# Order of work in a fused attention and expert kernel: gate weights, key and query steps, and the planning of slot 0

## The chip, the cores and the metric

One core of a Trainium2 chip runs the whole kernel. Five engines run their own queues in order: PE (TensorE, matrix products and transposes through the identity; PEld are its weight loads), ACT (ScalarE), DVE (VectorE), POOL (GpSimd) and SP (SyncE, which here only issues loads). The metric is the device time of one execution in microseconds; the time of a kernel is the median of several runs.

## The reference, cut to what matters

```
# attention: 4 batches x 8 heads, 768 tokens, 64 wide; 8 memory keys and values per head
for c in range(24):                              # chunks of 32 queries
    k_ctx = k[:, :, max(0, 32*c - 16):min(768, 32*c + 40)]
    scores = q_c @ concat(mem_k, k_ctx).T / 8
    a = softmax(scores)
    out[:, :, chunk] = a @ concat(mem_v, v_ctx)
# experts: the result as 3072 tokens x 512, 8 experts, one chosen per token
x = out.transpose(0, 2, 1, 3).reshape(3072, 512)
logits = x @ w_gate + modality_bias[modality_id]
e = argmax(logits); gate = softmax(logits)[e]
y[token] = gate * (relu(x[token] @ w1[e]) @ w2[e])    # 512 -> 1024 -> 512
```

Everything is float32. Expert products are made of a high and a low part of each operand (fp32r), three products for each full one.

## The kernel before, in words

**Attention.** The 32 heads are taken as 16 pairs u, each pair in two half steps, so 32 steps i = 2u + hf, in a loop that is pipelined by hand (`for i in range(n + 2)`). Step i issues the scores of its own unit (L328), transposes, attends (L345, L357) and normalizes (L365 to L370) the unit before, and transposes the result of the unit before that into `xall` (L382, L385). In between stands the preparation of the next pair. In an even step: `trans_k` of both heads on PE (L310, L314), four key copies `store_k` on ACT (L320), the memory keys on POOL (L302), and `regroup_q`, a DVE copy of the next pair's queries (L277). In an odd step: `trans_q` of both halves on PE (L292) with two copies on ACT (L297), and `share_v`, which copies value rows that two chunks share, on POOL (L267). POOL also issues the stores of the attention's result (`store_x`, L375).

**Loads.** SP issues every load in program order: keys and queries of a pair (L93), values of a pair in three pieces per head (L254 to L256), memory rows (L263), and once four small loads with the gate weights (L170 to L173). `gate_weights` spreads the gate weights over a padded tile `wg` on POOL (L234, L235), `bias_rows` makes the bias rows (L238 to L242).

**Routing.** After each four pairs the batch is routed (`route`): gate logits on PE (L530), their transposition (L541, L542), ranks by matmuls (L572 to L577), then six pairs of one-hot tiles ("hot tiles", `l` L656 and `a` L659), of which the first two are made on POOL and the others on DVE, and six matmuls of them (L667) that give the table of places (L671). The gates `gt` (L615) go to a DRAM tensor `gd`: by POOL (L622) for most batches, by SP (L1098) for the third, amid slot 0's weight loads. The route is a generator: each `yield "v"` ends a step after one DVE instruction, and `pump` or `further` take so many steps at places of the program, so that its instructions are mixed into the engines' queues by where these calls stand. Of the last batch's route (`last`, taken on by `further`) four of six tiles are made on POOL, and the gates' store stands ahead of the third tile.

**Experts.** A slot is 256 tokens of one expert: tokens are fetched by indirect DMA (`gather`, L751), transposed (`trans`: PE L803, high part on ACT L805, low part on DVE L806), weights are split into high (ACT L741) and low (DVE L742) by `conv`, the first product is `mm1_first` (L830, L831, L832) and the second `mm2` (L842). Slot 0's result is scaled on ACT (L846) and scattered by two indirect DMAs on POOL (`store`, L847); `keep` (L745, L747) puts the places and gates of the next slot aside on POOL. During slot 0 the last batch's route runs with `plan_slots`, a chain of small DVE instructions (L445 to L470, with `plan_row` L422 to L442 in it) that distributes the tokens over the later slots. The transposes of slot 1 stand in the second product of slot 0, at f = 5 and 6.

```
    for f in range(8):              # second product of slot 0
        if f == 2: further(2, True)
        mm2("av", f)
        if f < 5: conv(11 + f)
        if f == 5: load_w(1, 1)
        if f in (5, 6): trans(f - 5)
        if f > 2:
            further(2)
            conv(f - 3)
    store(0)
```

Of the kernel before, what the change touches and what calls it, by code (L numbers as in the profile page):

```python
# [39 lines left out]
NVW = 3  # L40
ORDERED = {mybir.EngineType.PE, mybir.EngineType.SP, mybir.EngineType.Pool, mybir.EngineType.Activation, mybir.EngineType.DVE}
# [3 lines left out]
def tile_chunk_attention_top1_moe(  # L45
# [239 lines left out]
    def trans_q(u):  # L285
        qr = qrs.pop(u)
        for j in range(2):
            t = qts[u, j] = bank()
            if u == 1 and j == 0:
                warm(t, 5)  # L290
            for i in range(3):
                nc.tensor.transpose(t[:, i:3 * P:3], qr[:, 2 * i + j].rearrange("p h d -> p (h d)"), ident)  # L292
# [11 lines left out]
    def trans_k(u):  # L304
        k2 = k2s.pop(u)
        for h in (1, 0):
            hh = 2 * u + h
            t = kts[u, h] = bank()
            for i in range(3):
                nc.tensor.transpose(t[:, 9 + i:9 + i + 3 * P:3], k2[:, 3 * h + i, :], ident)  # L310

            pads = bass.AP(tensor=t.tensor, offset=t.offset + 1, ap=[list(t.ap[0]), [392, 2], [1, 8]])
            mem_sel = ident[:, 4 * hh:4 * hh + 4].unsqueeze(1).unsqueeze(1)
            nc.tensor.matmul(pads, mkp, mem_sel.to_broadcast([P, 2, 2, 4]), start=True, stop=True)  # L314
# [107 lines left out]
    def plan_row(pos, tail, pt):  # L422
# [8 lines left out]
        vec.tensor_mul(three[:, 1], three[:, 1], noth)  # L431
        vec.scalar_tensor_tensor(off, off, 2.0, col0u, op0=ALU.mult, op1=ALU.add)
# [12 lines left out]
    def plan_slots():  # L445
# [21 lines left out]
        vec.reduce_sum(row, plan_row(pcol[0:64], None, None), axis=AX.X)  # L467
# [4 lines left out]
    def plan_tails():  # L472
# [28 lines left out]
        vec.reduce_sum(row, plan_row(pos, tail, pt), axis=AX.X)  # L501
# [453 lines left out]
    for i in range(n + 2):  # L955
# [26 lines left out]
        if u + 1 < NU and hf == 0:  # L982
# [3 lines left out]
            if 0 < u < NU - 2:  # L986
                regroup_q(u + 1)
# [11 lines left out]
        elif u + 1 < NU:  # L999
# [6 lines left out]
            trans_q(u + 1)  # L1006
            store_q(u + 1, 0)
            store_q(u + 1, 1)
            pump(3)
# [47 lines left out]
        if i == 9:  # L1057
            gate_weights()
            bias_rows()
        if i == 5:  # L1060
            nc.scalar.copy(mvx[1][:, :, 0:D], mvn[:, 1:2].to_broadcast([P, NCH, D]))
        if i == n - 5:
            regroup_q(NU - 1)
# [12 lines left out]
        if (u, hf) == (NU - 2, 1):  # L1076
# [20 lines left out]
            with nc.allow_non_contiguous_dma(reason="one gate per token"):  # L1097
                nc.sync.dma_start(*chosen.pop())  # L1098
# [57 lines left out]
    for f in range(8):  # L1156
# [9 lines left out]
        if f > 2:  # L1166
            further(2)
            conv(f - 3)
# [158 lines left out]
```

## Time and profile before

| what | value |
|---|---|
| runs, us | 427.58, 426.6, 427.71; median 427.58 |
| profiled execution, us | 428.59, of which its span is 426.8 |
| busy, us and share | PE 407.6 (95%), PEld 342.6 (80%), DVE 334.1 (78%), ACT 298.6 (70%), POOL 238.6 (56%) |
| granted clock, mean | 0.992 |
| attention | 9 to 131 us; from there on the expert slots |
| slot 0, slot 1 | first product of slot 1 from 163.8 us |

Times in the trace count from the span's start. A row of a timeline is a run of like instructions on one engine: its start, its length, the line, what it writes and reads, how many, and in brackets how long the engine stood idle ahead of it and what ended that. The granted clock (PEclk) is 1 at full speed, 2.4 GHz, and 0.5 at 1.2 GHz. A wait on one engine costs time only if the end of the program hangs on it, which must be followed from engine to engine.

### The profile page before, as it was taken

What the parts mean: (1) busy time and instruction counts of PE and PEld (TensorE: products, weight loads), DVE (VectorE), ACT (ScalarE), POOL (GpSimd) and SP (SyncE); (2) the same over time, 40 slices, a digit from 0 to 9 for tenths busy, and PEclk for the clock granted to TensorE, in tenths of its full rate; (3) what the DMA queues carried; (4) which work ended last, traced back from release to release, by engine and by line L of the source; (5) the groups of instructions that cost most, each with busy time, mean ns of one, the idle gap of its engine ahead of it and who ended that gap; (6) DMA issues with size and microseconds to landing.
All of it is one profiled execution on the core that took longest, in us unless ns stands there. A gap on an engine that the chain in (4) does not pass through costs nothing.

```text
span 426.8 us, 11396 instructions
## 1 busy us (share of the span) xinstructions
PE 407.6 (95%) x3872; PEld 342.6 (80%) x3875; DVE 334.1 (78%) x788; ACT 298.6 (70%) x594; POOL 238.6 (56%) x320
## 2 busy tenths in 40 slices
PE   8899699999899999999999999999999999999993
PEld 5678478888776888989898887888888788888882
DVE  6989468879687878958979889768789787988750
ACT  7677667868685556746657677868878676888750
POOL 8886567668583445767754574354666266520101
PEclk9999999999999999999999999999999999999998
DMA  9899899999957920125423729979776514320101
GB/s 221 146 261 228 193 235 210 223 239 192 232 156 201 271 52 1 55 77 121 99 78 72 272 64 266 290 231 297 231 282 196 157 54 102 73 77 2 50 3 55
DMA packets 82543, 66.81 MB, mean 157 GB/s; under 512 B 50659, under 2 KB 71339, under 8 KB 82476
## 3 DMA queue, kind: packets, MB, share of 16 engines
q1 hardware_dynamic: 75276, 46.36, 45.0%
q0 software_dynamic: 6784, 19.50, 15.0%
q8 instruction: 33, 0.54, 0.5%
q14 instruction: 34, 0.28, 0.2%
q10 hardware_dynamic: 416, 0.13, 0.1%
HBM read 84.64 MB, written 12.76 MB: 228 GB/s over the span
## 4 chain that ended last, share of the span: by engine, by line
PE 71%; issue 12%; ACT 6%; POOL 4%; DVE 4%; DMA 2%; POOLq 0%; ACTq 0%
PE av L842 12%; PE tr L830 11%; PE sc L842 10%; PE tr L811 9%; PE av L357 5%; PE tr L814 5%; ACT kbd L320 4%; PE sc L328 4%; PE tr L382 3%; PE tr L345 2%; PE tr L292 2%; PE tr L310 2%; PE tr L530 2%; DMA out_dram<-o,ix_now 1%; POOL xg L751 1%
## 5 line engine op out<-in xcount | busy, mean ns | idle before, releaser
L811 PE MATMUL tr<-xt,w 128*128 128x512 f32 x256 | 70.1, 395 | 0.0
L742 DVE TENSOR_TENSOR w<-raw,w 128x512 fp32r<-128x512 f32 x96 | 64.7, 719 | 4.0 <-ACT w L741 3.2
L842 PE MATMUL av<-wh,h 128*128 128x512 f32 x192 | 61.5, 393 | 0.0
L267 POOL COPY vw<-vw 24x1472 f32<-24x1472 f32 x31 | 44.2, 1425 | 21.8 <-DMA vw<-in_v_dram 20.6
L741 ACT CAST w<-raw 128x512 fp32r<-128x512 f32 x96 | 53.9, 623 | 1.5 <-DMA raw<-in_moe_w_dram 1.5
L842 PE MATMUL sc<-wh,h 128*128 128x512 f32 x160 | 50.8, 392 | 0.0
L811 PEld LDWEIGHTS tr<-xt,w 128*128 128x128 f32 x256 | 44.3, 189 | 7.2 <-issue 0.8
L830 PE MATMUL tr<-xt,w 128*128 128x256 f32 x384 | 48.1, 284 | 0.7 <-DVE xt L806 0.7
L830 PEld LDWEIGHTS tr<-xt,w 128*128 128x128 f32 x384 | 46.8, 191 | 2.0 <-DVE xt L806 1.0
L320 ACT COPY kbd<-tr 64x672 f32<-64x672 f32 x57 | 44.5, 781 | 4.3 <-DVE kbd L320 2.3
L814 PEld LDWEIGHTS tr<-xt,w 128*128 128x128 f32 x256 | 39.2, 189 | 5.4
L847 POOL DMA_INDIRECT out_dram<-o,ix_now x22 | 26.1, 1184 | 29.6 <-ACT o L846 24.3
L842 PEld LDWEIGHTS av<-wh,h 128*128 128x128 f32 x192 | 36.0, 188 | 7.5 <-issue 0.2
L814 PE MATMUL tr<-xt,w 128*128 128x256 f32 x256 | 40.7, 281 | 0.0
L820 DVE TENSOR_TENSOR hs<-tr,hs 128x256 f32<-128x256 f32 x64 | 26.8, 419 | 17.6 <-ACT hs L817 17.6
L842 PE MATMUL av<-wl,h 128*128 128x512 f32 x96 | 37.5, 390 | 0.0
L821 ACT ACTIVATE h<-hs 128x256 fp32r<-128x256 f32 x64 | 26.8, 419 | 14.8 <-DVE hs L820 13.7
L751 POOL DMA_INDIRECT xg<-gd,gx x24 | 27.1, 1128 | 14.7 <-DMA gd<-gt 9.0
L842 PEld LDWEIGHTS sc<-wh,h 128*128 128x128 f32 x160 | 30.0, 188 | 6.3 <-issue 0.2
L823 DVE TENSOR_TENSOR wl<-vw,wh 128x512 fp32r<-128x512 f32 x48 | 33.2, 691 | 2.2
L824 DVE SCALAR_TENSOR_TENSOR h<-hs,h 128x256 fp32r<-128x256 f32 x64 | 27.7, 433 | 7.7 <-ACT h L821 7.3
L776 POOL COPY planes<-xg 128x1024 uint16<-128x1024 uint16 x18 | 24.0, 1339 | 17.0 <-DMA xg<-xd,gx 16.9
(266 smaller groups left out, 910.4 us busy)
## 6 DMA issues: line engine op xcount, KB each, us to landing
raw<-in_moe_w_dram SPq DMA_DIRECT2D x96, 256.0 KB
vw<-in_moe_w_dram SPq DMA_DIRECT2D x72, 256.0 KB
k<-in_k_dram SPq DMA_DIRECT2D x16, 384.0 KB
q<-in_q_dram SPq DMA_DIRECT2D x16, 384.0 KB
xd<-xb POOLq DMA_DIRECT2D x16, 384.0 KB
kbd<-in_moe_w_dram SPq DMA_DIRECT2D x24, 256.0 KB
vw<-in_v_dram SPq DMA_DIRECT2D x32, 184.0 KB
xall<-in_moe_w_dram SPq DMA_DIRECT2D x4, 1024.0 KB
```

Of the source, the lines that this page charges most:

```text
L267: copy(vw[r0:r0 + 24, h, 1:NCH, 0:D], vw[r0 + 32:r0 + 56, h, 0:NCH - 1, 0:D])
L320: copy(dst.rearrange("p c (i j) -> p c i j", j=2)[:, :, :, j], win)
L741: nc.scalar.copy(wh[i], raw[i])
L742: (eng or nc.vector).tensor_sub(wl[i], raw[i], wh[i].bitcast(F32))
L751: nc.gpsimd.indirect_dma_start(out=xg[t][:, part], out_offset=None, in_=rows, in_offset=bass.IndirectOffsetOnAxis(ap=gx[:, t:t + 1], axis=0))
L811: nc.tensor.matmul(ph, wh[f][:, c * P:(c + 1) * P], xt[:, c].rearrange("p a n -> p (a n)"), start=(c == 0), stop=False, skip_group_check=True)
L814: nc.tensor.matmul(ph[:, 0:256], wl[f][:, c * P:(c + 1) * P], xth[:, c], start=False, stop=(c == 3), skip_group_check=True)
L820: nc.vector.tensor_add(hs, ph[:, 0:256], hs)
L823: nc.vector.tensor_sub(wl[w], raw[w], wh[w].bitcast(F32))
L824: nc.vector.scalar_tensor_tensor(hl[:, f], hs, 0.0, hh[:, f].bitcast(F32), op0=ALU.max, op1=ALU.subtract)
L830: nc.tensor.matmul(ph, w[f][:, c * P:(c + 1) * P], x[:, c, :], start=(n == 0), stop=(n == 11))
L842: nc.tensor.matmul(pos[t], x, w[8 + f], start=(f == 0 and n == 0), stop=(f == 7 and n == 2))
```

## The change

It has four parts.

1. `gate_weights` and `bias_rows` are called at the end of step 8 instead of step 9.
2. From pair 6 on (`AHEAD = 5`), each step prepares one half of keys and one half of queries. The even step 2u makes the transposes and two copies of head 1's keys and of the queries' half 0, all of pair u + 1. The odd step 2u + 1 makes the queries' half 1 of pair u + 1, then the keys of head 0 of pair u + 2 with two copies, and `regroup_q` of pair u + 2. On PE an even step before had L310 and L314 twice and an odd one L292 for both halves; after, each step has L310 and L314 once and L292 for one half.
3. In slot 0's second product: `plan_row` ends a step in its middle (for `plan_slots` alone); at f = 5 one step of the route is taken instead of two; the subtraction of weight block 1 goes to POOL; blocks 2 and 3 are both converted at f = 6.
4. In slot 0's start the third batch's gates are stored by POOL instead of SP.

```diff
@@ -38,6 +38,7 @@
 NPOOL = 2
 NSPIN = 8
 NVW = 3
+AHEAD = 5
 ORDERED = {mybir.EngineType.PE, mybir.EngineType.SP, mybir.EngineType.Pool, mybir.EngineType.Activation, mybir.EngineType.DVE}
 
 
@@ -282,9 +283,9 @@
         for _ in range(k):
             nc.tensor.matmul(t, idle[:, 0:P], idle[:, P:640], start=True, stop=True)
 
-    def trans_q(u):
-        qr = qrs.pop(u)
-        for j in range(2):
+    def trans_q(u, js=(0, 1)):
+        qr = qrs[u]
+        for j in js:
             t = qts[u, j] = bank()
             if u == 1 and j == 0:
                 warm(t, 5)
@@ -301,9 +302,9 @@
             r = slice(64 * h, 64 * h + 64)
             eng.tensor_copy(kbds[u % 2][r, :, h, 56:64], memT[r, u:u + 1, :].to_broadcast([64, NCH, NMEM]))
 
-    def trans_k(u):
-        k2 = k2s.pop(u)
-        for h in (1, 0):
+    def trans_k(u, hs=(1, 0)):
+        k2 = k2s[u]
+        for h in hs:
             hh = 2 * u + h
             t = kts[u, h] = bank()
             for i in range(3):
@@ -419,7 +420,7 @@
         nc.vector.tensor_scalar(t, t, MAGIC, -MAGIC, op0=ALU.add, op1=ALU.add)
         return t
 
-    def plan_row(pos, tail, pt):
+    def plan_row(pos, tail, pt, step=None):
 
         vec = nc.vector
         full, sta, end = plan["full"], plan["sta"], plan["end"]
@@ -429,6 +430,8 @@
         vec.scalar_tensor_tensor(isf, end, pos, isf, op0=ALU.is_gt, op1=ALU.mult)
         vec.scalar_tensor_tensor(three[:, 1], off, 0.0, isf, op0=ALU.is_equal, op1=ALU.mult)
         vec.tensor_mul(three[:, 1], three[:, 1], noth)
+        if step:
+            yield step
         vec.scalar_tensor_tensor(off, off, 2.0, col0u, op0=ALU.mult, op1=ALU.add)
         vec.tensor_mul(three[:, 2], off, isf)
         if tail is not None:
@@ -464,7 +467,8 @@
         vec.scalar_tensor_tensor(sta, ohg[0:64], 2.0, sta, op0=ALU.mult, op1=ALU.add)
         vec.tensor_add(end, sta, left)
         row = plan_new("row", 3)
-        vec.reduce_sum(row, plan_row(pcol[0:64], None, None), axis=AX.X)
+        parts = yield from plan_row(pcol[0:64], None, None, "v")
+        vec.reduce_sum(row, parts, axis=AX.X)
         yield "v"
         vec.tensor_scalar(row[:, 2:3], row[:, 2:3], float(E * HI), None, op0=ALU.add)
         vec.tensor_copy(regs1, row)
@@ -498,7 +502,8 @@
         vec.tensor_scalar(pos, nfull, -32.0, tail_row, op0=ALU.add, op1=ALU.mult)
         vec.tensor_add(pos, pos, pcol[0:64])
         row = plan_new("row", 3)
-        vec.reduce_sum(row, plan_row(pos, tail, pt), axis=AX.X)
+        parts = yield from plan_row(pos, tail, pt)
+        vec.reduce_sum(row, parts, axis=AX.X)
         vec.tensor_scalar(row[:, 2:3], row[:, 2:3], float(E * HI), None, op0=ALU.add)
         vec.tensor_copy(regs, row)
 
@@ -979,11 +984,21 @@
                 nc.vector.tensor_copy(memT.rearrange("p u m -> p (u m)"), memp[:, 0:P])
                 load_mv(2)
             pump(1)
-        if u + 1 < NU and hf == 0:
+        if AHEAD <= u < NU - 1 and hf == 0:
+            if u < NU - 2:
+                mem_keys(u + 1, nc.gpsimd)
+            trans_k(u + 1, (1,))
+            pump(1)
+            store_k(u + 1, 1, 0, nc.scalar.copy)
+            store_k(u + 1, 1, 1, nc.scalar.copy)
+            trans_q(u + 1, (0,))
+            store_q(u + 1, 0)
+            pump(1)
+        elif u + 1 < NU and hf == 0:
             if 0 < u < NU - 2:
                 mem_keys(u + 1, nc.gpsimd)
             trans_k(u + 1)
-            if 0 < u < NU - 2:
+            if 0 < u < AHEAD:
                 regroup_q(u + 1)
             if u == 1:
                 blank_v(2)
@@ -1003,9 +1018,17 @@
                 share(u + 1, 0, nc.gpsimd.tensor_copy)
             else:
                 share_v(u + 1)
-            trans_q(u + 1)
-            store_q(u + 1, 0)
+            if u < AHEAD:
+                trans_q(u + 1)
+                store_q(u + 1, 0)
+            else:
+                trans_q(u + 1, (1,))
             store_q(u + 1, 1)
+            if AHEAD <= u + 1 < NU - 1:
+                trans_k(u + 2, (0,))
+                store_k(u + 2, 0, 0, nc.scalar.copy)
+                store_k(u + 2, 0, 1, nc.scalar.copy)
+                regroup_q(u + 2)
             pump(3)
         elif live:
             pump(3)
@@ -1054,13 +1077,11 @@
                 routing.append((route(u2 // 4), "tiled", u2 // 4, i))
         for _ in range(4 if i > 2 and hf == 1 else 0):
             next(constants, None)
-        if i == 9:
+        if i == 8:
             gate_weights()
             bias_rows()
         if i == 5:
             nc.scalar.copy(mvx[1][:, :, 0:D], mvn[:, 1:2].to_broadcast([P, NCH, D]))
-        if i == n - 5:
-            regroup_q(NU - 1)
         if i < n:
             pump(1, ("tiled",))
         if i < 2:
@@ -1095,7 +1116,7 @@
                 nc.gpsimd.memset(raw[f][0:1, 0:1], 0.0)
             load_w(0, 0, 1)
             with nc.allow_non_contiguous_dma(reason="one gate per token"):
-                nc.sync.dma_start(*chosen.pop())
+                nc.gpsimd.dma_start(*chosen.pop())
         elif (u, hf) == (NU - 1, 1):
             other = second()
             for f in range(8, 16):
@@ -1164,8 +1185,12 @@
         if f in (5, 6):
             trans(f - 5)
         if f > 2:
-            further(2)
-            conv(f - 3)
+            further(1 if f == 5 else 2)
+        if f in (3, 4, 7):
+            conv(f - 3, nc.gpsimd if f == 4 else None)
+        if f == 6:
+            conv(2)
+            conv(3)
     store(0)
 
     tails = plan_tails()
```

POOL around the gate weights; L267 are the copies of value rows, L375 the stores of the result, L302 the memory keys. Before:

```order
L302 COPY kbd_111<-memT 64x24x8 x2
L267 COPY vw_114<-vw_114 24x23x64 x2
L375 DMA xd<-xb 128x6x128
L234 MEMSET wg_135 128x480
L235 COPY wg_135<-wg 128x12x8
L238 MEMSET mods 25x128
L239 CAST mods<-mod_i 24x128
L240 TENSOR_TENSOR bias_b<-bias_b 24x8
L242 TENSOR_TENSOR rows_b<-bias_b,ident 24x192
L302 COPY kbd_110<-memT 64x24x8 x2
```

After, where line numbers are one higher in this part:

```order
L376 DMA xd<-xb 128x6x128
L303 COPY kbd_111<-memT 64x24x8 x2
L235 MEMSET wg_135 128x480
L236 COPY wg_135<-wg 128x12x8
L239 MEMSET mods 25x128
L240 CAST mods<-mod_i 24x128
L241 TENSOR_TENSOR bias_b<-bias_b 24x8
L243 TENSOR_TENSOR rows_b<-bias_b,ident 24x192
L268 COPY vw_114<-vw_114 24x23x64 x2
L376 DMA xd<-xb 128x6x128
```

The six instructions on gate weights and bias have moved ahead of one pair's value copies and result store.

POOL in slots 0 and 1, from the first hot tiles of the last batch on (L847 the scatters of slot 0's result, L622 the gates' store). Before:

```order
L656 TENSOR_SCALAR l_3162<-iota_147,lo 128x130
L659 TENSOR_SCALAR a_3163<-iota_148,ac,tokm 128x192
L656 TENSOR_SCALAR l_3166<-iota_147,lo 128x130
L659 TENSOR_SCALAR a_3167<-iota_148,ac,tokm 128x192
L622 DMA gd<-gt 128x6x4
L656 TENSOR_SCALAR l_3200<-iota_147,lo 128x130
L659 TENSOR_SCALAR a_3201<-iota_148,ac,tokm 128x192
L656 TENSOR_SCALAR l_3204<-iota_147,lo 128x130
L659 TENSOR_SCALAR a_3205<-iota_148,ac,tokm 128x192
L847 DMA out_dram<-o_3213,ix_now_171 3072x512
L847 DMA out_dram<-o_3218,ix_now_171 3072x512
L745 COPY ix_now_172<-ix 128x2
```

After; L661 and L664 are the hot tiles, L852 the scatters, L750 and L752 the copies of `keep`, L627 the gates' store:

```order
L747 TENSOR_TENSOR w_2583<-raw_2587,w_2582 128x512
L661 TENSOR_SCALAR l_3175<-iota_147,lo 128x130
L664 TENSOR_SCALAR a_3176<-iota_148,ac,tokm 128x192
L661 TENSOR_SCALAR l_3179<-iota_147,lo 128x130
L664 TENSOR_SCALAR a_3180<-iota_148,ac,tokm 128x192
L852 DMA out_dram<-o_3199,ix_now_171 3072x512
L852 DMA out_dram<-o_3204,ix_now_171 3072x512
L750 COPY ix_now_172<-ix 128x2
L752 COPY gate_now_174<-xg_2579 128x1
L752 COPY gate_now_174<-xg_2580 128x1
L627 DMA gd<-gt 128x6x4
L661 TENSOR_SCALAR l_3246<-iota_147,lo 128x130
```

A subtraction of weights stands ahead of the first two tiles, and the scatters, the copies and the gates' store ahead of the other two. The six matmuls on PE that take the tiles have kept their place, between the seventh and the eighth block of slot 1's first product.

DVE in the same stretch, from the first half's low part of slot 1's tokens on. Before, the second half's low part (the second L806) follows behind the plan, the third tile's inputs L629 to L640 and a subtraction L742, 19 rows further on; its last rows:

```order
L629 TENSOR_SCALAR h_3155<-rank 128x3x2
L632 TENSOR_SCALAR hi<-h_3155 128x6
L636 SCALAR_TENSOR_TENSOR lo<-hi,rank 128x6
L640 TENSOR_TENSOR ac<-c_3001,hi 128x6
L742 TENSOR_TENSOR w_2583<-raw_2588,w_2582 128x512
L806 TENSOR_TENSOR xt<-tr,xt 128x2x256
L610 TENSOR_REDUCE s_3186<-rex 128x3x2
```

After, from the first to the second half's low part (L811 for L806):

```order
L811 TENSOR_TENSOR xt<-tr,xt 128x2x256
L467 SCALAR_TENSOR_TENSOR sta<-ohg,sta 64x8
L468 TENSOR_TENSOR end<-sta,left 64x8
L428 TENSOR_SCALAR isf<-sta,pcol 64x8
L429 TENSOR_SCALAR off<-sta,pcol 64x8
L430 SCALAR_TENSOR_TENSOR isf<-end,pcol,isf 64x8
L431 SCALAR_TENSOR_TENSOR three<-off,isf 64x8
L432 TENSOR_TENSOR three<-three,noth 64x8
L811 TENSOR_TENSOR xt<-tr,xt 128x2x256
L435 SCALAR_TENSOR_TENSOR off<-off,col0u 64x8
```

The second half's low part stands in the middle of `plan_row`, ten rows earlier than the inputs of the hot tiles.

## Rows read from the trace of the kernel before

**Rows 1.** Timeline of PE: start us, us, what (out<-in, count), idle before and releaser.

```profile
51.44 2.78 PE L530 MATMUL tr<-xall,wg 128*32 128x256 f32 x24 [3.08 <-POOL wg L235]
53.98 1.30 PE L328 MATMUL sc<-kbd,qT 128*32 128x128 f32 x24
```

**Rows 2.** Timeline of PE in the second batch's step, same columns.

```profile
82.56 1.48 PE L530 MATMUL tr<-xall,wg 128*32 128x256 f32 x24
```

**Rows 3.** Windows: busy time per engine, then PEclk, DMA share, GB/s.

```profile
51.40:54.90 3.50, 3.46 (x44) 2.15 (x48) 0.00 (x0) 0.37 (x1) 2.53 (x7) 0.51 1.11 246
```

**Rows 4.** Timeline of GpSimd (POOL) around the gate weights.

```profile
46.64 3.10 POOL L267 COPY vw<-vw 24x1472 f32<-24x1472 f32 x2 [4.22 <-DMA vw<-in_v_dram]
...
51.12 0.27 POOL L235 COPY wg<-wg 128x96 f32<-128x96 f32 x1
```

**Rows 5.** Waits in 57 to 131 us: total, times, longest.

```profile
PEld tr L292 <- ACT kbd L320: 3.9, 8, 1.0
```

**Rows 6.** Timeline of SP's queue: small loads, queries, values, memory rows.

```profile
41.19 0.81 SPq L173 DMA_DIRECT2D rows_b<-n_moe_modality_bias_dram  x1
...
61.89 1.43 SPq L93 DMA_DIRECT2D q<-in_q_dram  x1
...
108.22 0.39 SPq L93 DMA_DIRECT2D q<-in_q_dram  x1
...
110.37 0.33 SPq L254 DMA_DIRECT2D vw<-in_v_dram  x1
...
112.05 2.89 SPq L263 DMA_DIRECT2D vw<-mvx  x2
```

**Rows 7.** Timeline of GpSimd at the attention's end.

```profile
116.57 2.88 POOL L267 COPY vw<-vw 24x1472 f32<-24x1472 f32 x2
...
124.45 1.00 POOL L659 TENSOR_SCALAR a<-iota,ac,tokm 128x192 fp32r<-128x192 f32 x1
```

**Rows 8.** Timeline of PE at the attention's end.

```profile
122.42 0.84 PE L328 MATMUL sc<-kbd,qT 128*32 128x128 f32 x24
...
126.10 0.91 PE L667 MATMUL tr<-a,l 128*128 128x192 f32 x6
```

**Rows 9.** Timeline of DVE at slot 1's start.

```profile
165.08 0.68 DVE L806 TENSOR_TENSOR xt<-tr,xt 128x512 fp32r<-128x512 f32 x1
```

**Rows 10.** Timeline of ACT at slot 1's start.

```profile
162.52 0.59 ACT L805 CAST xt<-tr 128x512 fp32r<-128x512 f32 x1 [0.67 <-PE tr L803]
```

**Rows 11.** Timeline of GpSimd in slot 1, whole up to the copies of keep.

```profile
164.59 1.06 POOL L656 TENSOR_SCALAR l<-iota,lo 128x130 fp32r<-128x130 f32 x1 [9.32 <-DVE ac L640]
...
167.25 1.30 POOL L659 TENSOR_SCALAR a<-iota,ac,tokm 128x192 fp32r<-128x192 f32 x1
168.50 0.93 POOL L622 DMA_DIRECT2D gd<-gt  x1
169.48 0.62 POOL L656 TENSOR_SCALAR l<-iota,lo 128x130 fp32r<-128x130 f32 x1
...
172.26 1.32 POOL L659 TENSOR_SCALAR a<-iota,ac,tokm 128x192 fp32r<-128x192 f32 x1
173.76 1.46 POOL L847 DMA_INDIRECT out_dram<-o,ix_now  x1 [0.18 <-ACT wh L741]
175.53 1.44 POOL L847 DMA_INDIRECT out_dram<-o,ix_now  x1 [0.30 <-ACT h L831]
...
177.09 0.31 POOL L747 COPY gate_now<-xg 128x1 f32<-128x1 f32 x2
```

**Rows 12.** Timeline of PE in slot 1, as far as the second expert product.

```profile
165.82 9.13 PE L830 MATMUL tr<-xt,w 128*128 128x256 f32 x74 [0.74 <-DVE xt L806]
174.79 0.82 PE L667 MATMUL tr<-a,l 128*128 128x192 f32 x6
175.56 1.70 PE L830 MATMUL tr<-xt,w 128*128 128x256 f32 x12
```

**Rows 13.** Line 847 (the scatters): duration ns, least, middle and longest.

```profile
L847 POOL DMA_INDIRECT out_dram<-o,ix_now x22: 982/1042/2695, 173.8 to 399.9; - x22
```

## The prediction

> **What bounds the kernel now.** I read the table of engines first, then PE's timeline, then what PE waits for. From 165 us to the end of the expert layers PE is never idle for as much as half a microsecond but once, so whatever PE loses or gains there goes into the end time one to one. In the attention part (9 to 131 us) there is one large hole: the gate logits of the first batch (L530) start after 3.08 us of idle, waiting for the gate weights that GpSimd spreads out at L235 [rows 1]. The hole has a second half. In the 3.5 us behind it the granted clock is 0.51, the lower of the two levels, 1.2 GHz [rows 3]; the same logits take 2.78 us there and 1.48 us in the second batch, the scores behind them 1.30 us and elsewhere 0.84 us [rows 1, 2, 8]. So the hole costs 3.08 + 1.30 + 0.46 = 4.8 us where it stands, with a few tenths more in the transposes between: 5.0 us.
>
> Two other things pace the attention, and they decide what becomes of these 5.0 us. First the loads: SP issues the queries of pair 9 at 61.89 and those of pair 15 at 108.22, 46.33 us for six pairs, 7.72 us a pair [rows 6]. SP does so when the loads before have landed, not when PE has used something, so a faster PE does not bring them forward. Second GpSimd's queue at the end: copy of pair 14's value rows, then the first two hot tiles of the third batch, which end at 125.45, and at 126.10 PE's table matmuls L667 take them [rows 7, 8].
>
> **Gate weights one step earlier.** In before, L234 to L242 stand on GpSimd behind the value copies of pair 5, which waited 4.22 us for their load and ran until 49.74 [rows 4]. After, they stand ahead of these copies. The last of the small loads was issued by SP at 41.19 [rows 6]. If it takes no longer than queries do (6.1 us, next part), the six instructions, 2.1 us in the trace (50.56 to 52.64), could end at 49.4 at the latest, and by the size of the load far sooner; PE is ready for L530 at 51.44 - 3.08 = 48.36. I take it that they are ready in time. The copies of pair 5 may come up to 2.1 us later, and a result store behind them; the step that attends with them comes two steps behind the hole, so nobody waits. Local gain at L530: 5.0 us, of which the slow case would leave 4.
>
> **Where the gain goes.** Queries of pair 15 bound how far PE can be ahead at step 29: SP's second load of the memory rows (two in the row that starts at 112.05 and ends at 114.94, 0.65 us each) starts when they are in, at 114.3, that is 6.1 us after their issue [rows 6]. Regrouping, transposes and copies take 2.7 us more, so the scores at 122.42 [rows 8] may come at 117.0: PE keeps 5.4 us at most there, the 5.0 and what the loads leave of the second part. But PE then meets L667 of the third batch, and that waits for GpSimd. Pair 14's second value load was issued at 110.37; at the 6.1 us that the queries took it is there at 116.5, its copy ends at 117.9 instead of 119.45, 1.5 us earlier, and everything behind it on GpSimd (a store, the expert choice that SP's weight loads wait for, the hot tiles) is 1.5 us earlier too: hot tiles done at 123.95, L667 at 124.05 instead of 126.10. That is **a gain of 2.0 us**. If the load is no earlier than the copy shows, PE still takes L667 right at 125.45: 0.65 us. If GpSimd's chain did not bind: 5.4 us. I take 2.0, by the load next to it in the queue.
>
> **Keys and queries spread evenly.** PE and ACT do the same work in other steps. What it can free is PE's wait for the key copies in odd steps, 3.9 us in 57 to 131 [rows 5]. The even spread needs each pair's queries one step (3.5 us) sooner. As the loads set the pace, I cost it at nothing by itself: its gain stands under the 5.4 us above and is cut by GpSimd in the same way. If the loads did not hide it, up to 3.9 us.
>
> **Second tile's split amid the planning.** PE waits 0.74 us at 165.82 for DVE's split of the second half (L806 at 165.08), which stands behind the whole of the planning [rows 9, 12]. ACT's part of the split ends at 163.11 [rows 10], so L806 can now run at 163.11 to 163.79. The wait and its 0.2 us of weight loading go: **0.95 us gained**. The price is what has been queued past it. On DVE, L640 has the 0.7 us of L806 ahead of it [rows 9], and so the first hot tile, which started at 164.59 when L640 was done [rows 11], starts at 165.3. On GpSimd two hot tiles come first as before, but then both scatters of slot 0's result (L847) and the two copies of keep, then the gates' store, and only then hot tiles 2 and 3, for which L667 on PE waits, with slot 1's whole remainder behind it. Step by step, on before's time axis:
> - hot tiles 0 and 1: 3.96 us [rows 11], 165.3 to 169.3;
> - two scatters: 1.46 and 1.44 us there, with 0.3 between [rows 11], but 1.04 in the middle of all 22 [rows 13]; 2.1 to 3.2, I take 2.5, to 171.8;
> - copies 0.45, gates' store 0.93 [rows 11], to 173.2;
> - hot tiles 2 and 3: 4.10 us as they stand [rows 11]; but PE has stopped by then and DVE with it, and the shorter L656 took 0.62 [rows 11] and the shorter L659 1.00 [rows 7], 3.24 us for two tiles. I take 3.3, to 176.5.
>
> PE comes to L667 at 174.79 - 0.95 = 173.84 [rows 12], does two of six, and waits. Four of six are left, 4/6 of the 0.82 us of that row, 0.55: PE is back at its experts at 177.05, and was at 175.56 [rows 12]: **1.5 us lost, net of the 0.95 gained**. With all instructions at their shorter values (3.96, 2.1, 1.4, 3.24) the tiles end at 175.3 to 176.0 and the loss is 0.25 us at the least; with all at the longer ones they end at 177.95, and it is 2.95. The subtraction that goes to GpSimd stands ahead of the hot tiles, in 9.32 us of idle [rows 11], and PE needs it only at 165; I cost it at nothing. Were it as long as 3 us it would still end before 165.3.
>
> On the length of the tiles the trace shows 1.00 us for L659 at 124.45, in the attention, and 1.30 and 1.32 us at 167.25 and 172.26, where DVE subtracts weights [rows 7, 11]. The Trainium skill, page "SBUF — State Buffer", section "Who interferes with whom", says that a VectorE instruction with two inputs in SBUF and a GpSimd one that reads SBUF exclude each other, the later waiting. By that rule the subtractions still queued at 173 us would keep the longer values for tile 2, and the loss would be some 0.4 us more.
>
> **Gates' store on GpSimd in slot 0.** It leaves SP's queue between the weight loads and takes 0.93 us on GpSimd, like the store of [rows 11], between short memsets that free SP's next loads. No instruction of PE waits for these within several microseconds. Cost and gain: nothing; with that cover gone it would be GpSimd's 0.93 us against, and as much for SP's earlier loads.
>
> **Sum.** -2.0 + 1.5 = -0.5 us. The profiled execution took 428.59 us, 1.0 above the median of the runs, and 1.8 above its own span; by the profiled one the forecast is 428.1, by the median 427.58 it is **427.1**, and that is the number I give.
>
> **Rivals.**
> (a) Slower: GpSimd's queue in slot 1 keeps the longer values, PE stands for some 3.9 us in two pieces, and the clock falls as it did after 3.08 us in one piece [rows 1, 3]. Price: 2.95, and 3.5 x 0.49 = 1.7 for the clock [rows 3], less 2.0: +2.65, 430.2. It decides where PE's idle before L667 passes about 3 us, hot tile 3 ending after 177.2. For it: every duration in rows 11 is one of this place. Against it: a short piece of matmul lies between the two waits, and DVE runs dry. The Trainium skill, "TensorE: Matmul & The Clock Gate", Part 1, says that the array's clock is halved when PE has been little busy and comes back when it is busy again; by that rule the clock's loss is real only in a long wait, which is why this case carries it and the forecast does not. Chance 0.22.
> (b) Faster: GpSimd does not bind at 124 us because pair 14's values are there earlier than any row says, and the whole of PE's 5.4 us arrives. -5.4 + 1.5 = -3.9, 423.7. For it: the copies of pair 14 ran without a pause, so their load may have been there long before. Against it: the loads' pace of 7.72 us a pair. Chance 0.15.
> (c) The attention gives only 0.65 us: pair 14's load is as late as the copies allow. +0.85, 428.4. Chance 0.12.
> (d) The third part does what it says and no more, no new wait at L667: the scatters need GpSimd only for a fraction of the time their rows show. -2.0 - 0.95 = -2.95, 424.6. Against it: the rows' sums. Chance 0.10.
>
> **How the numbers follow.** The forecast, 427.1, has 0.41, with own ends of 1.25 below and 1.45 above by the bounds of scatters and tiles. About 0.3% (1.3 us) is what a measurement of this kernel can tell from no change. Of the forecast's 0.41, 0.11 fall under 426.3, 0.27 within, 0.03 above; (a) is slower but for 0.03; (b) faster; (c) within but for 0.03; (d) faster but for 0.01. Faster 0.11 + 0.15 + 0.09 = 0.35, slower 0.03 + 0.19 + 0.03 = 0.25, the same 0.40. The range reaches down to (b) and up to (a), 423.8 to 430.2, which leaves out about half of each of the two.
>
> **What the changed profile would show.** Right: L530 of the first batch without a wait and no low clock at 51 us; PE waits for GpSimd's L659, 2 to 3 us in all, at the third batch's L667 near 122 us; no wait for L806 at slot 1's start, and 2 to 3 us at the last L667, with L847 ahead of L656 on GpSimd. Wrong: no wait at either L667 (then b or d), a low granted clock at 175 us (a), or SP's cadence of pairs under 7.3 us, which would mean that PE and not the loads set it.

## The result, and the profile after

The changed kernel takes 428.12 us (median of 18 runs) where the kernel before takes 426.37 us in the same comparison (18 runs); the ratio is 1.0051, with a 95% interval of 1.0026 to 1.0076. It is **slower by about 2 us**: 2.2 by the ratio, 1.75 by the medians; the ratio is taken over the fast runs alone (it leaves out two of the changed kernel's 18), and is not the quotient of the medians. The forecast was 0.5 us faster. The profiled execution took 427.23 us, 1.4 us less than the profiled one of before, so the two profiles show the opposite of the medians. Single executions of one kernel differ by 3 us and more, and a stage has to be compared over several of them.

The page of the changed kernel; PEclk is the granted clock in 40 slices, tenths of full speed:

```profile
span 425.4 us, 11403 instructions
...
PE 407.5 (96%) x3875; PEld 345.6 (81%) x3875; DVE 340.6 (80%) x787; ACT 301.3 (71%) x594; POOL 239.4 (56%) x322
...
PEclk9899999999999999699999999999999999999999
```

The 6 in the middle is the slice around 175 us. The low clock at 51 us of [rows 3] is gone, and a longer one has come at slot 1.

First the hole that the first part was to close. PE's timeline at the gate logits (start us, us, what; no bracket: no wait), which answers to [rows 1, 2]:

```profile
48.46 1.48 PE L535 MATMUL tr<-xall,wg 128*32 128x256 f32 x24
```

GpSimd's timeline at the gate weights, which answers to [rows 4]:

```profile
42.67 0.26 POOL L236 COPY wg<-wg 128x96 f32<-128x96 f32 x1 [0.67 <-DMA wg<-in_moe_w_gate_dram]
```

The gate weights are spread 5.5 us before PE asks for them, and the logits run at full speed.

PE's timeline in slot 1, which answers to [rows 12], with the first product, the six table matmuls L672 (L667 before) and the start of the second product:

```profile
156.24 8.80 PE L835 MATMUL tr<-xt,w 128*128 128x256 f32 x72
165.40 1.68 PE L835 MATMUL tr<-xt,w 128*128 128x256 f32 x12 [0.36 <-DVE h L837]
167.41 0.44 PE L672 MATMUL tr<-a,l 128*128 128x192 f32 x2 [0.33 <-DVE h L837]
169.73 0.35 PE L672 MATMUL tr<-a,l 128*128 128x192 f32 x1 [1.88 <-POOL a L664]
171.31 0.95 PE L672 MATMUL tr<-a,l 128*128 128x192 f32 x3 [1.22 <-POOL a L664]
172.06 2.81 PE L835 MATMUL tr<-xt,w 128*128 128x256 f32 x12
174.67 0.63 PE L847 MATMUL sc<-wh,h 128*128 128x512 f32 x1
```

Before, slot 1's first product and its second product started here:

```profile
163.72 1.36 PE L830 MATMUL tr<-xt,w 128*128 128x256 f32 x10
...
177.09 0.40 PE L842 MATMUL sc<-wh,h 128*128 128x512 f32 x1
```

The wait of 0.74 us for L806 is gone, but PE waits 0.36 and 0.33 us for DVE's low parts of h (L837) instead, and comes to the table matmuls no earlier: 11.17 us after the slot's first matmul, before 11.07. There PE waits 1.88 and 1.22 us for GpSimd's tiles, and the block behind them takes 2.81 us, where [rows 12] has 1.70 for the same 12 matmuls. The windows say why (busy time of each engine in a stretch, then PEclk, DMA share, GB/s):

```profile
167.00:171.00 4.00, 0.87 (x4) 0.48 (x3) 3.06 (x7) 0.38 (x1) 3.94 (x5) 0.98 0.12 12
171.00:177.60 6.60, 6.29 (x22) 5.68 (x23) 2.90 (x6) 2.69 (x6) 3.63 (x6) 0.50 0.23 56
```

PE was busy for 0.87 of 4 us, and the 6.6 us behind that ran at 0.50, which is 1.2 GHz.

GpSimd's timeline in the same place, which answers to [rows 11]:

```profile
157.88 1.58 POOL L661 TENSOR_SCALAR l<-iota,lo 128x130 fp32r<-128x130 f32 x1 [7.72 <-DVE ac L645]
159.46 1.39 POOL L664 TENSOR_SCALAR a<-iota,ac,tokm 128x192 fp32r<-128x192 f32 x1
160.84 0.60 POOL L661 TENSOR_SCALAR l<-iota,lo 128x130 fp32r<-128x130 f32 x1
...
162.92 1.09 POOL L852 DMA_INDIRECT out_dram<-o,ix_now  x1 [0.17 <-issue]
164.31 1.57 POOL L852 DMA_INDIRECT out_dram<-o,ix_now  x1 [0.30 <-ACT wh L746]
...
166.25 0.92 POOL L627 DMA_DIRECT2D gd<-gt  x1
167.21 1.14 POOL L661 TENSOR_SCALAR l<-iota,lo 128x130 fp32r<-128x130 f32 x1
168.36 1.31 POOL L664 TENSOR_SCALAR a<-iota,ac,tokm 128x192 fp32r<-128x192 f32 x1
...
170.25 1.00 POOL L664 TENSOR_SCALAR a<-iota,ac,tokm 128x192 fp32r<-128x192 f32 x1
```

And DVE's timeline beside it:

```profile
157.76 1.29 DVE L747 TENSOR_TENSOR w<-raw,w 128x512 fp32r<-128x512 f32 x2
...
168.12 0.67 DVE L747 TENSOR_TENSOR wl<-vw,wh 128x512 fp32r<-128x512 f32 x1
...
169.05 0.67 DVE L747 TENSOR_TENSOR wl<-vw,wh 128x512 fp32r<-128x512 f32 x1
169.65 0.41 DVE L837 SCALAR_TENSOR_TENSOR h<-tr,h 128x256 fp32r<-128x256 f32 x1
```

From the start of the first tile to the end of the last GpSimd takes 13.4 us, and DVE goes on subtracting weights until 169.7 although PE has been standing since 167.85.

### The profile page after: what moved, and what is told of

The parts are those of the page before. It is cut to its first block, busy times and chain, and to the rows that moved or that the text cites. A ratio compares the mean times of both kernels' runs of the same rounds, so it can differ in the third digit from the quotient of the medians.

```text
span 425.4 us, 11403 instructions
## 1 busy us (share of the span) xinstructions
PE 407.5 (96%) x3875; PEld 345.6 (81%) x3875; DVE 340.6 (80%) x787; ACT 301.3 (71%) x594; POOL 239.4 (56%) x322
## 4 chain that ended last, share of the span: by engine, by line
PE 43%; issue 11%; POOL 5%; DMA 1%; ACT 1%; POOLq 0%; ACTq 0%
PE sc L847 11%; PE av L847 10%; PE tr L816 9%; PE tr L835 6%; PE tr L819 5%; DMA out_dram<-o,ix_now 1%; POOL xg L756 1%; PE tr L909 1%; PE tr L894 1%; POOL out_dram L852 1%; POOL planes L781 1%; POOL a L664 1%; POOL out_dram L1282 0%; POOL l L661 0%; ACT wh L746 0%
## 5 line engine op out<-in xcount | busy, mean ns | idle before, releaser
L747 DVE TENSOR_TENSOR w<-raw,w 128x512 fp32r<-128x512 f32 x95 | 67.4, 755 | 4.0 <-ACT w L746 3.6
L847 PE MATMUL av<-wh,h 128*128 128x512 f32 x192 | 61.5, 393 | 0.0
L847 PE MATMUL sc<-wh,h 128*128 128x512 f32 x160 | 51.9, 399 | 0.0
L835 PE MATMUL tr<-xt,w 128*128 128x256 f32 x384 | 49.2, 288 | 0.4 <-DVE h L837 0.4
L852 POOL DMA_INDIRECT out_dram<-o,ix_now x22 | 25.6, 1164 | 29.7 <-ACT o L851 24.3
L847 PEld LDWEIGHTS av<-wh,h 128*128 128x128 f32 x192 | 36.0, 188 | 7.5 <-issue 0.2
L819 PE MATMUL tr<-xt,w 128*128 128x256 f32 x256 | 40.7, 281 | 0.0
L825 DVE TENSOR_TENSOR hs<-tr,hs 128x256 f32<-128x256 f32 x64 | 26.8, 419 | 13.4 <-ACT hs L822 13.3
L847 PE MATMUL av<-wl,h 128*128 128x512 f32 x96 | 37.5, 390 | 0.0
L847 PEld LDWEIGHTS sc<-wh,h 128*128 128x128 f32 x160 | 30.8, 192 | 6.6 <-issue 0.2
L756 POOL DMA_INDIRECT xg<-xd,gx x24 | 28.0, 1166 | 13.8 <-PE tr L808 6.2
```

Of the source, the lines that this page charges most:

```text
L747: (eng or nc.vector).tensor_sub(wl[i], raw[i], wh[i].bitcast(F32))
L756: nc.gpsimd.indirect_dma_start(out=xg[t][:, part], out_offset=None, in_=rows, in_offset=bass.IndirectOffsetOnAxis(ap=gx[:, t:t + 1], axis=0))
L819: nc.tensor.matmul(ph[:, 0:256], wl[f][:, c * P:(c + 1) * P], xth[:, c], start=False, stop=(c == 3), skip_group_check=True)
L835: nc.tensor.matmul(ph, w[f][:, c * P:(c + 1) * P], x[:, c, :], start=(n == 0), stop=(n == 11))
L847: nc.tensor.matmul(pos[t], x, w[8 + f], start=(f == 0 and n == 0), stop=(f == 7 and n == 2))
L852: return nc.gpsimd.indirect_dma_start(out=out, out_offset=bass.IndirectOffsetOnAxis(ap=ix, axis=0), in_=o, in_offset=None, bounds_check=N ...
```

## The experiments

Two theories stood at the start. **Theory 1**: the queue on GpSimd in slot 1 costs 4 to 6 us (the wait and the clock behind it), more than the attention gains. **Theory 2**: that wait belongs to one execution, and the slower medians come from the attention. The table has every comparison, each with runs of the kernel before that belong to it; 1% is 4.26 us.

| kernel | runs | median, us | before, us | ratio, 95% interval |
|---|---|---|---|---|
| changed kernel, first | 18 | 428.12 | 426.37 | 1.0051, 1.0026 to 1.0076 |
| changed kernel, again | 12 | 428.26 | 426.14 | 1.0053, 1.0023 to 1.0082 |
| split alone | 6 | 432.99 | 426.04 | 1.0154, 1.0095 to 1.0213 |
| all tiles ahead of the scatters | 12 | 423.46 | 426.04 | 0.9947, 0.9908 to 0.9987 |
| the same, tiles 2 and 3 on DVE | 12 | 423.76 | 426.14 | 0.9939, 0.9907 to 0.9971 |
| without the split | 12 | 422.31 | 426.04 | 0.9928, 0.9894 to 0.9963 |
| without the split, again | 6 | 421.49 | 426.50 | 0.9897, 0.9849 to 0.9945 |
| gate weights and even steps alone | 6 | 421.48 | 426.50 | 0.9883, 0.9839 to 0.9927 |
| gate weights alone | 12 | 422.99 | 426.04 | 0.9927, 0.9895 to 0.9959 |
| gate weights alone, again | 12 | 423.53 | 426.50 | 0.9948, 0.9914 to 0.9981 |
| even steps alone | 12 | 423.63 | 426.14 | 0.9942, 0.9908 to 0.9975 |
| even steps alone, again | 12 | 423.76 | 426.50 | 0.9936, 0.9903 to 0.9968 |
| changed kernel, PE kept busy in the wait | 12 | 426.15 | 426.14 | 0.9981, 0.9943 to 1.0019 |

**The split alone.** The kernel before with the third part of the change and nothing else:

```diff
-            further(2)
-            conv(f - 3)
+            further(1 if f == 5 else 2)
+        if f in (3, 4, 7):
+            conv(f - 3, nc.gpsimd if f == 4 else None)
+        if f == 6:
+            conv(2)
+            conv(3)
...
+        if step:
+            yield step
```

> The kernel before with the third part of the change alone (split of the second tile amid the planning, one step of the route fewer, one subtraction on GpSimd). Theory 1, the queue on GpSimd: hot tiles 2 and 3 stand behind scatters, copies and gates' store, PE waits about 3.4 us at the last L672 and the clock falls for about 6 us behind it, as in the profile of the changed kernel: 3.9 us for the wait net of the 0.95 us gained, about 2.3 us for the clock, so 4 to 6 us slower, 1.0% to 1.4%. Theory 2, what the medians show comes from the attention and slot 1's wait is only this execution's: within 1 us of the kernel before.

It is 1.5% slower (0.95% to 2.1%), some 6.6 us. PE's timeline at the last table matmuls (L671 here):

```profile
173.23 0.44 PE L671 MATMUL tr<-a,l 128*128 128x192 f32 x2 [0.32 <-DVE h L836]
175.55 0.52 PE L671 MATMUL tr<-a,l 128*128 128x192 f32 x1 [1.88 <-POOL a L663]
177.12 0.95 PE L671 MATMUL tr<-a,l 128*128 128x192 f32 x3 [1.05 <-POOL a L663]
```

And the window behind them:

```profile
175.00:182.50 7.50, 5.90 (x21) 5.27 (x22) 2.86 (x7) 1.77 (x4) 4.42 (x7) 0.54 0.09 18
```

The waits of the changed kernel are here again with an attention that is not changed, and so is the low clock. Theory 2 falls.

**All tiles ahead of the scatters.** The changed kernel with two steps of the route more before the end of slot 0:

```diff
-            further(1 if f == 5 else 2)
+            further((2, 2, 1, 3, 3)[f - 3])
```

> The changed kernel with one step of the route more at each of the last two blocks of slot 0's second product, so that all hot tiles and the gates' store stand ahead of the scatters on GpSimd as in the kernel before, while the second tile's split stays amid the planning. Theory 1: no wait at the last L672, no low clock behind it; the attention's gain remains whole, 4 to 7 us, and the 0.95 us of the split comes on top: 1.0% to 1.8% faster than before. Theory 2: as slow as the changed kernel, 0.5% slower than before.

0.5% faster than before, and so 1% faster than the changed kernel, by two numbers in a list. PE's timeline at the last table matmuls:

```profile
172.49 0.55 PE L672 MATMUL tr<-a,l 128*128 128x192 f32 x3
173.88 0.58 PE L672 MATMUL tr<-a,l 128*128 128x192 f32 x3 [0.84 <-POOL a L664]
```

The window around them:

```profile
173.00:175.00 2.00, 1.16 (x10) 1.12 (x10) 2.00 (x5) 0.00 (x0) 1.82 (x2) 1.00 0.04 8
```

One wait of 0.84 us is left, and the clock stays at full speed. The expectation was 1.0% to 1.8%; the split's own 0.95 us does not show beside the kernel without it, for the reason given above: in this profile too PE waits for DVE's low parts of h instead, 0.26 and 0.23 us.

**Without the split.** The first, second and fourth part alone: the loop and `plan_row` of the kernel before, the rest as changed.

> The changed kernel without its third part: gate weights, even steps and gates' store on GpSimd alone. Theory 1: the attention's gain alone, 4 to 7 us, 0.9% to 1.6% faster than before, and 0.5 to 1 us slower than the kernel with all tiles ahead of the scatters. Theory 2: 0.5% slower than before, like the changed kernel.

0.7% faster, and 1.0% in a second comparison:

> Gate weights, even spread and the gates' store on GpSimd, once more; first time 0.72% faster than before (0.4% to 1.1%). If the store on GpSimd costs nothing, as I predicted: equal to the kernel with the two others alone. If it costs: 0.3% or more behind it.

So the third part is what makes the change slower: 1.0051 against 0.9928 and 0.9897.

**Tiles 2 and 3 on DVE.** The kernel with the tiles ahead, with

```diff
-        npool = 4 if b == B - 1 else NPOOL
+        npool = NPOOL
```

> The kernel with all tiles ahead of the scatters (label tiles), in which tiles 2 and 3 of the last batch are made on DVE as the tiles 4 and 5 are, instead of on GpSimd. GpSimd's queue holds only two tiles and the gates' store, and DVE gets about 1.6 us more to do. If the 0.84 us that PE still waited for GpSimd's tiles with all of them ahead is what keeps the split's gain away: no wait there, 1 us better than the kernel without the split, 0.9% faster than before. If DVE becomes the late one: PE waits for DVE's tiles or its h low parts, as fast as or slower than without the split (0.7% faster than before or less).

0.6% faster than before: no better than GpSimd's tiles ahead of the scatters and no better than no split. Its profile has no wait for a tile any more, but four waits of PE of 0.25 to 0.57 us for DVE's low parts of h. The second outcome holds: DVE is the late one then.

**PE kept busy in the wait.** The changed kernel with

```diff
         tb = bank()
+        if b == B - 1:
+            warm(tb, 16)
         for t, (l1, a1) in enumerate(hot):
```

> The changed kernel with 16 matmuls of no use (bf16, 0.27 us each in the trace, 4.3 us) on PE ahead of the last L672, in the time in which PE otherwise waits for GpSimd's tiles. They leave the wait as it is and keep PE busy in it. If the clock behind the wait is a price of its own: no low clock at slot 1, and of the 6.8 us at half speed of the changed kernel's profile some 3.2 us come back: from 0.5% slower to 0.2% or 0.3% faster than before. If the wait alone is the price: still about 0.5% slower, or worse where the 16 take longer than the wait.

PE's timeline from the useless matmuls on:

```profile
166.46 3.61 PE L284 MATMUL tr<-idle 128*128 128x512 bf16 x16 [0.23 <-DVE h L839]
169.72 1.30 PE L674 MATMUL tr<-a,l 128*128 128x192 f32 x6
170.87 1.62 PE L837 MATMUL tr<-xt,w 128*128 128x256 f32 x12
```

The window around them:

```profile
166.00:171.50 5.50, 5.20 (x30) 3.13 (x30) 3.56 (x9) 0.39 (x1) 4.34 (x5) 1.00 0.13 22
```

The useless matmuls fill the wait nearly to its end (GpSimd's last tile ends at 170.40), the block behind takes 1.62 us instead of 2.81, and the kernel comes from 0.5% slower (the changed kernel once more, next) to 0.2% faster, an interval that holds zero. The clock's share of the loss is 0.7% by these ratios, some 3 us, or 2.1 us by the medians (428.26 and 426.15); by the intervals it is uncertain by about 2 us. The wait's share is the rest.

**The changed kernel once more**, on the chip of that comparison:

> The changed kernel once more, on the same chip as the kernel with the useless matmuls: 0.3% to 0.8% slower than before, with a wait of 3 to 4 us at the last L672 and a low clock behind it. If the low clock was chance in the first profile, it is missing here.

0.53% slower, waits of 1.88 and 1.22 us again. The windows behind them:

```profile
174.00:177.00 3.00, 3.00 (x16) 3.00 (x17) 0.71 (x2) 0.07 (x1) 1.36 (x3) 0.60 0.03 5
177.00:180.00 3.00, 3.00 (x12) 2.36 (x12) 2.57 (x5) 3.00 (x7) 2.36 (x3) 0.83 0.56 143
```

The clock is low again, for (0.40 + 0.17) x 3 / 0.5 = 3.4 us by these means, half as long as in the first profile. It was low in all three profiled executions that had this wait (this one, the first and the split alone) and at full speed there in those of the kernels without it.

**Slot 1 in all the profiles.** Single executions differ mostly ahead of slot 1, so the profiles can be compared stage by stage from slot 1's first matmul on (us; the last column runs to the end of the span):

| kernel | to the table matmuls | to the second product | from there to the end |
|---|---|---|---|
| without the third part, eight profiles | 11.07 to 11.09 | 13.37 to 13.38 | 249.1 to 249.7 |
| split alone | 11.18 | 18.44 | 250.4 |
| changed kernel, first | 11.17 | 18.43 | 250.7 |
| changed kernel, again | 11.19 | 17.87 | 250.1 |
| PE kept busy in the wait | 14.35 | 16.95 | 249.4 |
| all tiles ahead of the scatters | 11.16 | 14.42 | 249.7 |
| the same, tiles 2 and 3 on DVE | 12.06 | 14.82 | 249.5 |

Beside the kernels without it (13.4 and, in the mean, 249.4), the third part costs 5.2 to 6.4 us, 5.9 in the mean of the three. With PE kept busy it costs 3.6. So by the profiles the wait's share is 3.6 us and the clock's 2.3, and these two do not hang on the medians of the runs. And in no form does the third part gain anything: even with all tiles ahead slot 1's first product ends 1.0 us later than without it.

**The two parts in the attention.** Gate weights alone (`if i == 8:` for `if i == 9:`), twice:

> The kernel before with the gate weights in step 8 alone. My prediction's account, loads at a pace of their own and GpSimd's chain at the end: 5.0 us gained at L530, of which 2.0 arrive, 0.5% faster. If the loads follow a faster PE, as the cadence of 7.2 us a pair in the changed kernel's profile suggests against 7.7 before: 3 to 5 us, 0.8% to 1.2% faster. If the attention's gain needs the even steps as well: under 1 us.

> The kernel with the gate weights in step 8 alone, once more, to compare it on one chip with the even spread alone and with both. First time: 0.73% faster than before (0.4% to 1.1%). If that stands: 0.5% to 0.9%.

0.73% and 0.52%, 2.7 us in the mean, uncertain by 1 us by the intervals. That lies between the prediction's account (2.0) and that of loads that follow PE (3 to 5), and decides for neither. The even steps alone (`AHEAD` and all that goes with it), twice:

> The kernel before with the even spread of keys and queries from the sixth pair on alone. If the loads or GpSimd set the pace of the attention, as I predicted, or if the spread is worth little by itself: within 0.3% of before. If it frees the waits of PE for key copies (3.9 us in 57 to 131): 0.5% to 0.9% faster.

> The kernel with the even spread alone, once more. First time 0.58% faster than before (0.25% to 0.9%), where I had costed it at nothing. If it stands: 0.4% to 0.8%; if it was chance: under 0.3%.

0.58% and 0.64%, 2.6 us in the mean, where I had put nothing. And the two together without anything else:

> Gate weights in step 8 and the even spread, nothing else (the gates' store on SP as before). If the two gains add: 1.1% to 1.5% faster than before. If they meet a common bound (pace of the loads, or PE wholly busy): 0.6% to 0.9%, as with the gates' store on GpSimd.

1.17% (0.7% to 1.6%), 5 us; with the gates' store on GpSimd beside them 0.72% and 1.03%. The gains add up for the most part; the mean of the three kernels with both is 0.97%, 4.1 us, against 5.3 for the sum. The store on GpSimd can't be told from nothing by these.

The profiles of the even steps alone, which still have the gate weights in step 9, show the hole of [rows 1] at other lengths. PE's timeline at the logits in the first profile:

```profile
51.07 2.62 PE L535 MATMUL tr<-xall,wg 128*32 128x256 f32 x24 [2.33 <-POOL wg L236]
```

The same row of the second:

```profile
50.73 1.50 PE L535 MATMUL tr<-xall,wg 128*32 128x256 f32 x24 [0.67 <-POOL wg L236]
```

With 2.33 us of wait the logits ran at the low clock, with 0.67 they did not. The split alone, whose attention is that of before, has a hole as large as the 3.08 us of [rows 1]:

```profile
50.05 2.79 PE L534 MATMUL tr<-xall,wg 128*32 128x256 f32 x24 [3.00 <-POOL wg L235]
```

So the hole differs between executions of the even steps. That it does so in the kernel before, and that this is why the gate weights bring 2.7 us and not 5.0, is not shown; where the rest goes stays open.

## Why the prediction was wrong

The sign failed at the price of the third part. It stands in the sum at +1.5 us and measured about 6 (6.6 by the split alone, 5.9 by the profiles of slot 1). Three things were wrong in that term: the 0.95 us gained at L806 never reached the table matmuls, the tiles took 13.4 us instead of 11.2, and the low clock behind the wait stands in the sum at nothing. The attention's term failed too, but the other way: -2.0 us, and 4.1 us gained, which hid part of the loss.

**Gate weights in time: right.** L236 runs at 42.67, the logits start without a wait and take 1.48 us, and no low clock follows. Locally the 5.0 us are there.

**Where the gain goes: wrong.** The step that failed here is GpSimd's chain at the attention's end, which I hung on the load of pair 14's values. GpSimd's timeline of the changed kernel, which answers to [rows 7]:

```profile
108.61 0.74 POOL L303 COPY kbd<-memT 64x192 f32<-64x192 f32 x2 [2.43 <-PE sc L329]
109.41 3.09 POOL L268 COPY vw<-vw 24x1472 f32<-24x1472 f32 x2
...
117.08 1.00 POOL L664 TENSOR_SCALAR a<-iota,ac,tokm 128x192 fp32r<-128x192 f32 x1
```

PE's timeline there, which answers to [rows 8]:

```profile
118.11 0.91 PE L672 MATMUL tr<-a,l 128*128 128x192 f32 x6
```

The copies of pair 14 stand behind the memory keys, and these wait 2.43 us for PE's scores. The values were there before. So GpSimd's chain hung on PE here and moved with it, and the wait of 2 to 3 us at L672 that the prediction named as a sign is missing. It was so in the kernel before already; this is the row ahead of the copies of [rows 7]:

```profile
115.77 0.75 POOL L302 COPY kbd<-memT 64x192 f32<-64x192 f32 x2 [3.41 <-PE sc L328]
```

The row that I gave the copies (no pause ahead of them) could not tell that: the instruction ahead of them in the queue is the one to look at. The load is not far off, though: in two other profiles with the same attention (all tiles ahead, and tiles 2 and 3 on DVE) the copies did wait for their values, 0.93 and 1.22 us in all. L672 came 8.0 us earlier than L667 of [rows 8] in this pair of profiles, but a single pair says little: in the split alone, with the attention of before, it came at 123.78. The mean is 124.9 in the two profiles with the attention of before and 120.3 in the eight with both parts, 4.6 us earlier; the medians have 4.1 for the end time.

**Loads at their own pace: only partly.** SP's queries of pair 9 and pair 15, which answer to [rows 6]:

```profile
58.48 0.63 SPq L94 DMA_DIRECT2D q<-in_q_dram  x1
...
102.14 0.40 SPq L94 DMA_DIRECT2D q<-in_q_dram  x1
```

43.7 us for six pairs, 7.28 us a pair against 7.72, just under the 7.3 that I had named as the sign. By the same rows it is 7.66 in the split alone, and from 7.22 to 7.56 in the twelve profiles that have one or both of the attention's parts (7.56 in the changed kernel's second one). So the loads came faster when PE was faster, but under 7.3 only in four of the twelve. What exactly made room for them was not tried. They do bind in places: with both parts and nothing else PE stood once for keys, and the stretch behind ran at a lower clock (0.83 over the 10 us from 53):

```profile
53.07 0.52 PE L311 MATMUL tr<-ident,k 128*128 128x128 f32 x3 [1.87 <-DMA k<-in_k_dram]
```

**Even steps at nothing: wrong by 2.6 us.** The upper end that I gave, the 3.9 us of [rows 5], was the nearer one. In the profiles of the even steps the wait of L293 for key copies is gone from PE's list of waits in 57 to 117 us; others for ACT and DVE have come (the logits' 0.6 us behind ACT in the third batch among them). That these are why 2.6 and not 3.9 arrive is argued, not tried.

**The split: right in its mechanism, wrong in its sizes.** The queue's order, the place of the wait and the end of the wait for L806 were as foretold. But the 0.95 us did not arrive: PE waits 0.69 us for low parts of h in place of the 0.74 for L806, and L672 starts 11.17 us after the slot's first matmul where the sum had 10.12. And the tiles were mis-sized: I put 11.2 us from the first tile to the last, they took 13.4. Tiles 0 and 1 took 4.9 us instead of 3.96, because the two subtractions that the change puts together (blocks 2 and 3) run at just that moment on DVE: the first L661 took 1.58 us, where it took 1.06 beside one subtraction [rows 11] and the second, which began beside none, took 0.60. And "PE has stopped by then and DVE with it" was false: DVE had two more weight subtractions to do after PE had stopped (at 168.12 and 169.05), and tile 2 took 1.14 + 1.31 us; only the last L664 ran at 1.00. The rule of the Trainium skill ("SBUF — State Buffer", "Who interferes with whom") that a two-input VectorE instruction and a GpSimd one that reads SBUF exclude each other was the better guide here, and the trace agrees with it for GpSimd: the tile that began at 157.88 ended 0.4 us after the subtractions that ended at 159.05, and the one that began at 168.36, inside the subtraction that ended at 168.79, ended 0.88 us after it, where alone it takes 1.00. It does not agree for DVE: the subtraction that began at 169.05, inside that tile, took its usual 0.67 us. By the comparison of the kernel kept busy in the wait (0.9981) with those without the split (mean 0.9903) the wait costs 3.3 us net, and 3.6 by the profiles of slot 1, against the 1.5 predicted and the 2.95 at the upper end.

**The clock: the forecast left it out, rival (a) had it.** On before's axis the last tile ended at 178.7 (13.4 us after the 165.3 at which the forecast has the first one start), beyond the 177.2 that the prediction named as the point. So (a), to which I gave 0.22, is what happened in slot 1: +2.65 us by its sum, 2.2 measured. That the two are so near is luck. Its parts are larger than it had them, and they cancel: attention -4.1 instead of -2.0, wait +3.3 instead of +2.95, clock +3.0 instead of +1.7 (2.3 by the profiles). The attention came nearer to (b)'s 5.4 than to the forecast's 2.0, as GpSimd hardly bound there. The two rivals stood side by side as if only one could come true, and both did in good part. (a)'s argument against itself, that a short piece of matmul between the two waits might hold the clock, did not hold in any of the three executions. The Trainium skill ("TensorE: Matmul & The Clock Gate", Part 1) has the array's clock halved when PE has been little busy, and the trace agrees: 0.87 us busy of 4, then 0.50.

The parts -4.1, +3.3 and +3.0 add up to the 2.2 us by construction, as each is the difference of two ratios of the table; it is no proof of them. What speaks for them independently is the split alone (6.6 us against 3.3 + 3.0) and the profiles of slot 1 (3.6 + 2.3). The kernel with both parts of the attention and without the third beats both: 1.0% faster than before, in the mean of three comparisons.

## What to carry to other kernels

A generator that is taken on by counted steps places work on every engine it touches: one step taken fewer and one added in `plan_row` moved two tiles on GpSimd behind two scatters, and PE, on another engine, waited for them; look at each engine's order before and after, and follow the last thing that a matmul on the path needs. Before a wait is booked at its own length, ask whether it empties PE long enough to lower the clock: here that cost 2 to 3 us beside the wait's own 3.3 to 3.6. Before the end of a wait is booked as a gain, ask what PE waits for next: here it was DVE again, for nearly as long. And ahead of an instruction that does not wait, look at the one before it in its queue; that one's wait tells what the chain hangs on.

## What the runs showed of the hardware

The clock fell behind waits that I took for too short or too broken. In the split alone PE stood from 173.67 on, and of the 7.5 us from 175.0 the mean clock was 0.54, although one table matmul ran between the two waits of 1.88 and 1.05 us. How long it stays low differs: 6.6 us in the first profile of the changed kernel, about half of that in the second, with the same waits. A GpSimd tile L661 that began inside one of DVE's weight subtractions took 1.14 us, and 1.58 inside two, where it takes 0.60 otherwise, in the same kernel and the same slot; the subtractions beside the tiles kept their 0.67 to 0.69 us. And the hole in front of the first logits, 3.08 and 3.00 us in two executions with the attention of before, was 2.33 and 0.67 us in two of the even steps alone.
